# A pooled attention and a gated convolutional FFN on one core: the whole written-out order of operations is replaced

## The chip, the core and the metric

The kernel runs on one core of one Trainium2 chip. The metric is the device time of one execution in microseconds. The engines are TensorE (PE; its weight loads are listed as PEld), VectorE (DVE), ScalarE (ACT), GpSimd (POOL) and SyncE (SP). Each runs its own instructions strictly in the order in which the program issued them, and waits on semaphores for the others.

## The reference

There are 8 batches of 576 rows, 8 heads of 64. Keys and values are averaged over groups of 8 rows, so that 576 queries meet 72 pooled keys. The attention's output (576 x 512 a batch) goes through a feed-forward layer whose hidden activation (1024 wide) is multiplied by a sigmoid gate, which is a three-tap convolution along the sequence.

```python
k_p = k.reshape(B, H, Sp, pool, D).mean(axis=3)
v_p = v.reshape(B, H, Sp, pool, D).mean(axis=3)
scores = scale * np.matmul(q, k_p.transpose(0, 1, 3, 2))
attn = softmax(scores)                       # over 72 keys
x = np.matmul(attn, v_p)                     # heads side by side: 576 x 512
h = np.maximum(x @ w_in, 0.0)                # 576 x 1024
conv_out = sum(conv_w[k] * hp[:, k:k + S, :] for k in range(3))
out = (h * sigmoid(conv_out)) @ w_out        # 576 x 512
```

## The kernel before, in words

Batches go in pairs, the groups g = 0 to 3 (batches 2g and 2g + 1), and a group's 1152 rows are cut into tiles t of 128 rows (tile 4 holds the seam of both batches; group 0 has two halves of it, tiles 4 and 9). POOL issues all loads of inputs and weights: `load_q` and `load_k` (L272), `load_v` (L290 and a rest at L293), `load_pair` for the keys of a whole group (L279), `load_w_in` in two halves (L300) and `load_w_out` (L308). SP and ACT issue the stores, and SP the transposing DMAs.

One attention tile is a chain over the engines: scores on PE (`att_scores`, L567 in a form of 64 x 64 tiles, or L580), the negative maximum on DVE (L593), the shift by it (DVE L605, or for group 0 PE L613), exp on ACT (L631), the turning of e (on PE, L642, with a copy, L656; from group 2 on by a transposing DMA that SP issues, L651), the values on PE (`att_values`, L667), the division on DVE (L680, L682), and the turning into xT (PE L699 and a copy, L707, or a DMA, L691).

One batch's FFN has, for each of eight blocks of 128 hidden columns, the first product on PE (`ffn_in`, L712), relu on ACT (L721), the convolution (either on PE by diagonal matrices, L874, or as three taps, ACT L847 and DVE L849), tanh on ACT (L854, L899), the gate and its product with h on DVE (L860, L861, L910, L912, L920), then the second product (`ffn_out`, L928), a copy out of PSUM (L939, DVE or ACT) and the store (L951).

Before the first tile, PE averages and turns batch 0's keys with a pool matrix (L391; the matrix is made by DVE memsets at L327 to L329, two POOL selects at L316 and a DVE copy at L332) and turns its queries (L501). For later groups DVE sums the key pair in three halving steps (`pool_pair`, L424) and the values in three steps and a masked product (L471, L475).

The function builds a list of 1013 operations with their dependences, but decides nothing about their order. That is written out in three tables in the class `Graph`. `ORDER` holds one number for each operation in the order of issue: the half of it is the operation's index, the lowest bit chooses the first or the second engine that it may use, and -1 is a filler, a matmul of 448 columns on a blank tile whose result nobody reads (L384). `FORMS` chooses between two tilings of some score and turning operations on PE. `PLACES` gives each use of a ring of buffers (PSUM banks, e, eT, v, qp and others) its slot. The operations are emitted in that order, and so every engine's queue is a subsequence of it:

```python
for n in self.ORDER:
    o = spares.pop(0) if n < 0 else self.ops[n // 2]
    o.engine = list(o.engines)[0 if n < 0 else n % 2]
```

Of the kernel before, what the change touches and what calls it, by code (L numbers as in the profile page):

```python
# [33 lines left out]
class Graph:  # L34
# [88 lines left out]
    )  # L123
    FORMS = (
        1, 1, 0, 0, 0, 1, 1, 0, 0, 0, 0, 0, 1, 1, 1, 0, 0, 0, 0, 0, 0, 1, 1, 0, 0, 0, 0, 0, 0, 0, 0, 1, 1, 1, 0, 1, 1, 1, 1, 1,
    )
    PLACES = (
# [1265 lines left out]
```

## Time and profile before

| what | value |
|---|---|
| median of 3 runs | 222.53 us (221.14 to 223.88) |
| the profiled execution | span 224.8 us; no time beside the span is shown |
| PE busy | 205.1 us, 91% |
| DVE busy | 195.4 us, 87% |
| ACT busy | 160.9 us, 72% |
| POOL busy | 45.1 us, 20% |
| mean granted TensorE clock | 0.979 |

A busy time is the union of an engine's instructions. Matmuls are pipelined and their ends are modelled, so a busy PE need not be at its peak. "Idle before" in a group's row is the time for which its engine stood ahead of it, with what ended that; "issue" is a wait for nothing that the profile shows. The granted clock is that of TensorE, where 1 is full speed.

### The profile page before, as it was taken

The numbers are of one execution on the slowest core, as the hardware profiler recorded it, in microseconds if no ns is written. First come the engines' busy times: TensorE is split into PE (matmuls) and PEld (weight loads), VectorE is DVE, ScalarE is ACT, GpSimd is POOL, SyncE is SP. The second block draws the span as 40 slices with busy tenths as digits, with TensorE's granted clock in tenths as the row PEclk, the third lists the DMA queues.
The fourth block names the chain that finished last, engine by engine and source line by source line (L and its number), as shares of the span: only waits on it lengthen the run. The fifth ranks groups of instructions, "written<-read, shape, count | busy, mean of one in ns | idle before, by whom it ended". The sixth has DMA issues, their size and how long they took to land.

```text
span 224.8 us, 6558 instructions
## 1 busy us (share of the span) xinstructions
PE 205.1 (91%) x2722; PEld 137.9 (61%) x2722; DVE 195.4 (87%) x337; ACT 160.9 (72%) x271; POOL 45.1 (20%) x81
## 2 busy tenths in 40 slices
PE   5897999979999999959999949989999999999991
PEld 1465778755788877636677735656656665654450
DVE  7889876999999999957999948999999999999641
ACT  2155768898999958844697935688889999997210
POOL 7943321131230120000000121001031230540000
PEclk9999999999999999988999988999999999999997
DMA  5999999999999999947664553168566617423495
GB/s 81 137 191 207 207 206 208 207 207 206 207 208 206 155 187 172 207 39 163 121 106 92 119 118 76 32 92 165 117 145 140 137 23 166 95 48 71 96 247 194
DMA packets 48833, 32.61 MB, mean 145 GB/s; under 512 B 28300, under 2 KB 44324, under 8 KB 48804
## 3 DMA queue, kind: packets, MB, share of 16 engines
q0 software_dynamic: 16288, 16.26, 44.8%
q1 hardware_dynamic: 31796, 14.96, 33.3%
q10 hardware_dynamic: 720, 0.98, 1.5%
q8 instruction: 21, 0.34, 0.6%
q14 instruction: 8, 0.07, 0.1%
HBM read 32.52 MB, written 9.44 MB: 187 GB/s over the span
## 4 chain that ended last, share of the span: by engine, by line
PE 44%; DVE 30%; DMA 8%; issue 7%; ACT 6%; POOL 3%; DVEq 0%; POOLq 0%
PE psum L928 21%; PE psum L712 14%; DVE negm L593 6%; DMA qp<-in_q_dram 6%; DVE x L682 5%; DVE sd L605 5%; PE psum L874 4%; DVE tg L849 2%; DVE gT L912 2%; PE psum L667 2%; DMA eT<-e 2%; DVE v L471 2%; DVE r L680 2%; DVE gT L920 2%; ACT e L631 1%
## 5 line engine op out<-in xcount | busy, mean ns | idle before, releaser
L712 PE MATMUL psum<-xT,w_in_sb 128*128 128x288 bf16 x512 | 74.4, 289 | 0.8 <-ACT tg L899 0.5
L928 PE MATMUL psum<-w_out_sb,gT 128*128 128x512 bf16 (+1 forms) x296 | 70.3, 378 | 0.5 <-DVE gT L920 0.5
L712 PEld LDWEIGHTS <-w_in_sb 128*128 128x128 bf16 x512 | 48.4, 99 | 17.6 <-issue 1.6
L721 ACT ACTIVATE hT<-psum 128x576 bf16<-128x576 f32 x64 | 40.1, 652 | 14.9 <-PE psum L712 14.3
L928 PEld LDWEIGHTS <-gT 128*128 128x128 bf16 x296 | 27.7, 98 | 27.0 <-issue 1.2
L849 DVE SCALAR_TENSOR_TENSOR tg<-hT,convw,tg 128x576 f32<-128x576 bf16 x48 | 37.3, 818 | 0.4
L593 DVE TENSOR_REDUCE negm<-psum 128x8 f32<-128x576 f32 (+2 forms) x37 | 27.4, 750 | 4.4 <-PE psum L567 3.9
L796 POOL COPY hT<-hT 128x126 bf16<-128x126 bf16 x16 | 9.1, 567 | 101.4 <-ACT hT L721 90.9
L682 DVE TENSOR_TENSOR x<-psum,r 128x512 bf16<-128x512 f32 (+1 forms) x37 | 25.6, 691 | 1.3
L667 PE MATMUL psum<-vm,eT 128*128 128x130 bf16 (+5 forms) x240 | 20.0, 227 | 4.1 <-DMA eT<-e 2.9
L874 PE MATMUL psum<-hT,dw 64*64 64x288 bf16 (+2 forms) x608 | 19.2, 261 | 2.6 <-issue 2.3
L667 PEld LDWEIGHTS <-eT 128*128 128x128 bf16 (+1 forms) x240 | 16.0, 103 | 9.1 <-DMA eT<-e 3.8
L605 DVE TENSOR_TENSOR sd<-psum,negm 128x576 f32<-128x576 f32 x27 | 20.1, 752 | 1.0 <-ACT e L631 0.5
L631 ACT ACTIVATE e<-sd 128x576 bf16<-128x576 f32 x27 | 18.6, 689 | 1.8 <-DVE sd L605 1.6
L874 PEld LDWEIGHTS <-dw 64*64 64x64 bf16 x608 | 14.8, 107 | 7.6 <-issue 6.7
L847 ACT ACTIVATE tg<-hT,convw 128x576 f32<-128x576 bf16 x24 | 18.0, 773 | 1.0 <-DVE gT L912 0.9
L899 ACT ACTIVATE tg<-psum 128x576 bf16<-128x576 f32 x20 | 13.0, 653 | 7.2 <-PE psum L874 7.2
L939 ACT COPY osb<-psum 128x512 f32<-128x512 f32 x25 | 14.5, 586 | 4.0 <-PE psum L928 3.9
L854 ACT ACTIVATE gT<-tg 128x576 bf16<-128x576 f32 x24 | 16.2, 685 | 0.8 <-DVE tg L849 0.3
L471 DVE TENSOR_TENSOR v<-v 128x1280 bf16<-128x1280 bf16 (+2 forms) x24 | 13.0, 540 | 2.1 <-DMA v<-in_v_dram 1.9
L899 ACT ACTIVATE gT<-psum 128x576 bf16<-128x576 f32 x20 | 12.9, 649 | 2.0 <-PE psum L874 2.0
L920 DVE TENSOR_TENSOR gT<-gT,hT 128x2304 bf16<-128x2304 bf16 x10 | 13.5, 1349 | 0.0
(82 smaller groups left out, 236.2 us busy)
## 6 DMA issues: line engine op xcount, KB each, us to landing
out_dram<-osb SPq DMA_DIRECT2D x54, 128.0 KB, 2.4
v<-in_v_dram POOLq DMA_DIRECT2D x8, 512.0 KB, 15.2
qp<-in_q_dram POOLq DMA_DIRECT2D x7, 576.0 KB, 16.9
kk<-in_k_dram POOLq DMA_DIRECT2D x3, 1152.0 KB, 17.6
out_dram<-qp SPq DMA_DIRECT2D x10, 128.0 KB, 2.9
w_in_sb<-in_moe_w_in_dram POOLq DMA_DIRECT2D x2, 512.0 KB, 17.3
w_out_sb<-in_moe_w_out_dram POOLq DMA_DIRECT2D x1, 1024.0 KB, 24.3
out_dram<-qp ACTq DMA_DIRECT2D x6, 128.0 KB, 2.7
```

Of the source, the lines that this page charges most:

```text
L593: nc.vector.tensor_reduce(out=a["m"][0:rows], in_=a["s"][0:rows, :, 0:2 * KW].rearrange("p a (h s) -> p a h s", s=Sp), axis=AX.X, op=OP.ma ...
L605: nc.vector.tensor_tensor(out=a["d"][0:rows], in0=a["s"][0:rows, :, 0:2 * KW].rearrange("p a (h s) -> p a h s", s=Sp), in1=a["m"][0:rows]. ...
L631: nc.scalar.activation(out=dst, in_=src, func=ACT.Exp, scale=1.0 / (POOL * 8.0),)
L667: nc.tensor.matmul(out=a["o"][lo:hi, h // 4, (h % 4) * (D + 1):(h % 4 + x1 - x0) * (D + 1)], lhsT=a["eT"][:, j, lo:hi], rhs=buf("vm", b)[: ...
L682: nc.vector.tensor_tensor(out=a["x"][0:rows].rearrange("p (a h d) -> p a h d", a=2, d=D), in0=ov[:, :, :, 0:D], in1=r[0:rows].unsqueeze(3) ...
L712: nc.tensor.matmul(out=banks(ps)[:, j, 0:SC], lhsT=w_in_block(dc, fb), rhs=buf("xT", g)[:, dc, i * S + j * SC:i * S + (j + 1) * SC], start ...
L721: nc.scalar.activation(out=h_of(b)[:, fb].rearrange("p (a s) -> p a s", a=2), in_=banks(ps)[:, :, 0:SC], func=ACT.Relu, scale=0.5,)
L847: nc.scalar.activation(out=acc, in_=h, func=ACT.Identity, scale=w)
L849: nc.vector.scalar_tensor_tensor(out=acc, in0=h, scalar=w, in1=acc, op0=OP.mult, op1=OP.add)
L874: nc.tensor.matmul(out=banks(pss[r ^ c])[c * D:(c + 1) * D, j, lo:hi], lhsT=dw[r * D:(r + 1) * D, tap * n_fb + fb, :], rhs=hT[r * D:(r + 1 ...
L899: nc.scalar.activation(out=t.rearrange("p (a s) -> p a s", a=2), in_=banks(ps)[:, :, 0:SC], func=ACT.Tanh, scale=0.5,)
L928: nc.tensor.matmul(out=bank(ps)[0:rows, columns], lhsT=buf("gT", g)[:, fb, t * P:t * P + rows], rhs=w_out_sb[:, fb, columns], start=(fb == 0),
```

## The change

Only the three tables are replaced. The same 1013 operations are issued in another order; 15 stand at the place in the list that they had (fillers not counted), and the mean shift is 21 places, the largest 167. 28 copies change between DVE and ACT (17 from DVE to ACT, 11 back), and 7 stores between SP and ACT. 22 fillers become 2. In `FORMS`, one more turning of queries and one more score operation use the small tiling. All line numbers move up by 18, since the tables are shorter: L712 is now L694, and so on. The first rows of `ORDER` and the whole of `FORMS`:

```diff
     ORDER = (
-        18, 24, 2, 6, 4, 8, 10, -1, 16, -1, 14, -1, 20, 22, 12, -1, 42, -1, 44, -1,
-        -1, 34, 28, -1, 36, -1, -1, 30, 32, -1, 92, 0, 96, 98, 38, 95, -1, 56, 26, 104,
+        6, 10, 2, 4, 28, 16, 14, 20, 24, 22, 34, 8, 26, 42, 36, 44, 12, 32, 30, 40, 92, 56, 18, 98, 38, 95, 58, 101, 104, 64,
+        97, 108, 103, 106, 50, -1, 110, 54, 48, 302, 282, 60, 116, 304, 112, 119, 284, 306, 114, 286, 308, -1, 288, 322, 342, 324, 310, 66, 344, 326,
...
     FORMS = (
-        1, 1, 0, 0, 0, 1, 1, 0, 0, 0, 0, 0, 1, 1, 1, 0, 0, 0, 0, 0, 0, 1, 1, 0, 0, 0, 0, 0, 0, 0, 0, 1, 1, 1, 0, 1, 1, 1, 1, 1,
+        1, 1, 0, 0, 0, 1, 1, 1, 0, 1, 0, 1, 0, 1, 1, 0, 0, 0, 0, 0, 1, 1, 0, 0, 0, 0, 1, 1, 1, 1, 0, 0, 1, 0, 1, 0, 1, 0, 1, 0,
...
```

What this moves is seen in the queues of the engines. First POOL's loads after those of batch 0, before. The names are buffers: qp holds a batch's queries (qp1 to qp3 here batches 1 to 3, the qp0 below them batch 4), kk keys, v values of one batch, w_in_sb0 and 1 the halves of w_in.

```order
L272 DMA qp1_73<-in_q_dram 128x4x576
L272 DMA qp2_74<-in_q_dram 128x4x576
L300 DMA w_in_sb0_66<-in_moe_w_in_dram 128x4x512
L300 DMA w_in_sb1_67<-in_moe_w_in_dram 128x4x512
L290 DMA v1_86<-in_v_dram 128x4x512
L293 DMA v1_86<-in_v_dram 64x512
L279 DMA kk0_76<-in_k_dram 128x9x512
L272 DMA qp3_75<-in_q_dram 128x4x576
L272 DMA qp0_72<-in_q_dram 128x4x576
L308 DMA w_out_sb_68<-in_moe_w_out_dram 128x8x512
L290 DMA v2_87<-in_v_dram 128x4x512
L293 DMA v2_87<-in_v_dram 64x512
```

And now:

```order
L254 DMA qp1_73<-in_q_dram 128x4x576
L254 DMA qp2_74<-in_q_dram 128x4x576
L282 DMA w_in_sb1_67<-in_moe_w_in_dram 128x4x512
L282 DMA w_in_sb0_66<-in_moe_w_in_dram 128x4x512
L272 DMA v1_86<-in_v_dram 128x4x512
L275 DMA v1_86<-in_v_dram 64x512
L272 DMA v2_87<-in_v_dram 128x4x512
L275 DMA v2_87<-in_v_dram 64x512
L261 DMA kk0_76<-in_k_dram 128x9x512
L254 DMA qp0_72<-in_q_dram 128x4x576
L254 DMA qp1_73<-in_q_dram 128x4x576
L290 DMA w_out_sb_68<-in_moe_w_out_dram 128x8x512
```

Batch 2's values have moved ahead of the key pair of group 1 (kk0), of the queries of batches 4 (qp0) and 3 (now in qp1, and behind batch 4's) and of w_out; the halves of w_in have changed places.

Next PE's queue ahead of the values of tile (2, 5), group 2's tile 5. Of runs of equal rows the first is shown. xT0 is group 2's input to the FFN, eT its turned exponentials. Before, after the values of tile (2, 6), which read eT1; those of tile (2, 5) read eT0:

```order
L667 MATMUL psum_61<-vm0_88,eT1_103 128x65
L712 MATMUL psum_61<-xT0_112,w_in_sb1_67 128x288
L712 MATMUL psum_61<-xT0_112,w_in_sb0_66 128x288
L667 MATMUL psum_61<-vm0_88,eT2_104 128x130
L667 MATMUL psum_61<-vm0_88,eT0_102 128x130
```

And now, after the values of tile (2, 7); those of tile (2, 5) read eT2:

```order
L694 MATMUL psum_61<-xT1_113,w_in_sb1_67 128x288
L694 MATMUL psum_61<-xT0_112,w_in_sb1_67 128x288
L856 MATMUL psum_61<-hT0_114,dw_71 64x288
L549 MATMUL psum_61<-kT2_82,qT2_79 64x72
L910 MATMUL psum_61<-w_out_sb_68,gT0_119 128x512
L649 MATMUL psum_61<-vm0_88,eT0_102 128x130
L649 MATMUL psum_61<-vm1_89,eT2_104 128x130
```

Where two tiles' values stood next to each other behind some products of one batch, the values of tile (2, 5) now come behind products of two batches, a convolution, scores of group 3, output products and the values of a tile of group 3. Counted from the tile's own scores to its values, PE had 36 L712 matmuls and two tiles' values to do; now it has 72 of them (L694), 16 of L928 (L910), four convolution groups (128 matmuls of L874, now L856), 48 matmuls of scores and four tiles' values. The shortest such stretch of a tile of groups 2 and 3 is now that of tile (3, 1): 20 of L712, 16 of L928, one convolution group of 24 and 32 score matmuls.

Last, PE's start, before:

```order
L384 LDWEIGHTS gT1_120
L384 MATMUL psum_61<-gT1_120 128x448
L365 MATMUL psum_61<-gT1_120 128x24
L391 LDWEIGHTS kk0_76
L391 MATMUL psum_61<-gT1_120,kk0_76 64x144
```

And now:

```order
L347 MATMUL psum_61<-gT1_120 128x24
L373 LDWEIGHTS kk0_76
L373 MATMUL psum_61<-gT1_120,kk0_76 64x144
L483 LDWEIGHTS qp0_72
L483 MATMUL psum_61<-ident_62,qp0_72 64x128
```

Eleven fillers (L384) stood ahead of the first key matmul (L391) and eleven more came later; now none stands ahead of it, and the two that are left come after the first turnings of queries (L483) and among the first tiles' shifts.

116 rows, old and new, of tables (ORDER, PLACES) are left out of this document.

## The prediction

> **What bounds the kernel now.** I read the page first: busy shares and the chain that ended last.
>
> ```profile
> span 224.8 us, 6558 instructions
> PE 205.1 (91%) x2722; PEld 137.9 (61%) x2722; DVE 195.4 (87%) x337; ACT 160.9 (72%) x271; POOL 45.1 (20%) x81
> PE 44%; DVE 30%; DMA 8%; issue 7%; ACT 6%; POOL 3%; DVEq 0%; POOLq 0%
> ```
>
> TensorE (PE) is busy for 91% and VectorE (DVE) for 87%, and both carry the chain. The order of the work can only win what these two lose by waiting for each other or for transfers. Where that is, the busy time of each engine in seven stretches tells. After the stretch and its length come the busy times, the granted TensorE clock, the DMA share and GB/s.
>
> ```profile
> core 0: us, PE busy (x) PEld busy (x) DVE busy (x) ACT busy (x) POOL busy (x), PEclk, DMA share, GB/s
> 0.00:28.00 28.00, 22.05 (x387) 14.46 (x390) 23.63 (x59) 12.89 (x21) 16.18 (x33) 1.00 1.06 165
> 28.00:95.30 67.30, 64.83 (x1119) 49.37 (x1106) 62.77 (x113) 57.48 (x100) 11.84 (x17) 1.00 1.21 198
> 95.30:104.40 9.10, 6.81 (x97) 3.96 (x100) 5.13 (x9) 3.59 (x8) 0.00 (x0) 0.81 0.52 74
> 104.40:125.20 20.80, 20.63 (x400) 15.28 (x388) 20.26 (x38) 15.87 (x28) 0.00 (x0) 1.00 0.60 115
> 125.20:145.10 19.90, 17.02 (x187) 11.40 (x176) 15.62 (x26) 12.50 (x21) 3.32 (x8) 0.91 0.45 94
> 145.10:216.10 71.00, 70.09 (x574) 41.21 (x563) 65.68 (x93) 57.98 (x98) 13.77 (x24) 1.00 0.52 113
> ```
>
> In three of them both engines are nearly full (PE 64.83 of 67.30, 20.63 of 20.80 and 70.09 of 71.00): no order wins much there. The loss sits in the start, and in two short stretches where PE stands and the granted clock is below 1. The waits of PE between 90 and 140 us name two gaps, with the total, the times and the longest:
>
> ```profile
> PE psum L667 <- DMA eT<-e: 2.9, 1, 2.9
> PE psum L874 <- issue: 2.3, 1, 2.3
> ```
>
> The same table, cut finely around them, shows that a gap costs more than its length:
>
> ```profile
> 92.59:96.01 3.42, 3.42 (x80) 2.17 (x78) 3.29 (x5) 2.62 (x6) 0.00 (x0) 1.00 1.06 181
> 96.01:99.42 3.41, 1.12 (x35) 0.83 (x34) 0.65 (x2) 1.00 (x2) 0.00 (x0) 1.00 0.63 35
> 99.42:102.84 3.42, 3.42 (x16) 1.74 (x15) 2.70 (x5) 1.28 (x4) 0.00 (x0) 0.50 0.17 34
> 130.14:133.55 3.41, 0.54 (x8) 0.34 (x5) 1.11 (x2) 0.98 (x2) 1.26 (x2) 1.00 0.60 131
> 133.55:136.97 3.42, 3.41 (x18) 2.42 (x19) 2.47 (x5) 0.00 (x0) 0.00 (x0) 0.50 0.30 60
> 48.22:51.63 3.41, 2.50 (x62) 1.56 (x64) 3.38 (x5) 3.37 (x7) 0.77 (x1) 1.00 1.23 206
> ```
>
> PE was busy for 1.12 of 3.41 us, and then for 0.54 of 3.41 us, and each time the next 3.41 us ran at a clock of 0.50. Such a half-speed stretch does 1.7 us less work. So the first gap costs 2.3 + 1.7 = 4.0 us and the second 2.9 + 1.7 = 4.6 us. A stretch with 2.50 of 3.41 us busy (48.22) was followed by no loss of clock.
>
> By the Trainium skill, "TensorE: Matmul & The Clock Gate", Part 1, the clock halves after an idle window of about 3.4 us, and the windows run freely. The trace agrees, with 3413 ns to the window.
>
> **The change, part by part.** All 1013 planned operations stay; their order, their buffers, 35 choices of engine and some tiling forms change. Of 22 filler matmuls on PE 2 stay. The sum is made against the profiled execution's 224.8 us. Its row shows nothing around the span, and it is 1.0% above the median of the timed runs (222.53), so I scale the result by 0.990.
>
> *(a) The start without fillers.* The fillers take 7.8 us of PE, beside DVE's start and the first loads.
>
> ```profile
> L384 PE MATMUL psum<-gT 128*128 128x448 bf16 x22 | 7.8, 463 | 2.8 <-DVE gT L1027 2.5 <-ACT eT L656 0.2
> 4.08 3.17 PE L384 MATMUL psum<-gT 128*128 128x448 bf16 x8
> 8.32 1.32 PE L391 MATMUL psum<-gT,kk 128*64 128x144 bf16 x36 [1.07 <-DVE gT L332]
> 9.86 0.64 PE L501 MATMUL psum<-ident,qp 128*64 128x128 bf16 x16
> 10.43 0.55 PE L384 MATMUL psum<-gT 128*128 128x448 bf16 x2
> ```
>
> Eight early ones took 3.17 us (0.40 each), two later ones 0.55 (0.28 each): the early ones ran slowly and the key and query work after them did not. Without them L391 (1.32 us) and L501 (0.64) are the first long work and may take twice that, +2.0 us. Against it, DVE clears the pool matrix first and four other buffers earlier, so that L332 may come sooner; PE waited 1.1 us for it, and no more can be won. I take +0.8, between -1.1 and +2.0.
>
> The same page puts the warm-up at about 3.4 us at half speed, whatever is issued. By that alone this term would be +1.7 and the result 0.9 us later.
>
> *(b) The load queue.* Batch 2's values now go ahead of the key pair of batches 2 and 3.
>
> ```profile
> 28.00:40.00 12.00, 11.94 (x207) 9.60 (x197) 8.71 (x20) 8.72 (x16) 3.03 (x5) 1.00 1.24 207
> 20.64 1.03 POOL L279 DMA_DIRECT2D kk<-in_k_dram  x1 [4.75 <-PE psum L401]
> kk<-in_k_dram POOLq DMA_DIRECT2D x1, 1152.0 KB, 17.8
> 39.46 1.35 DVE L424 TENSOR_TENSOR kk<-kk 128x2304 bf16<-128x2304 bf16 x1
> ```
>
> The pair lands at 20.64 + 17.8 = 38.4 us, and DVE sums it at 39.46. Batch 2's 576 KB take 2.8 us at 207 GB/s, so it lands at 41.2 now: DVE waits up to 1.8 us at the head of its queue, with the scores' maxima behind it. But v2's own four operations now stand ahead of that sum and fill part of the wait. I take the middle, +0.9, between 0 and +1.8.
>
> *(c) The transposing DMA of tile (2, 5).* This is the second gap; the two rows of x4 are from the chain's listing, the others from the timeline.
>
> ```profile
> 124.95 0.32 PE L567 MATMUL psum<-kT,qT 64*64 64x72 bf16 x16
> 129.13 1.22 SPq L651 DMA_TRANSPOSE eT<-e  x1
> 133.56 0.84 PE L667 MATMUL psum<-vm,eT 128*128 128x130 bf16 x6 [2.88 <-DMA eT<-e]
> 34.12 0.49 PE psum L712 x4
> 82.21 0.86 PE psum L928 x4
> 124.14 0.94 PE L874 MATMUL psum<-hT,dw 64*64 64x288 bf16 x32
> 127.35 0.52 PE L667 MATMUL psum<-vm,eT 128*128 128x130 bf16 x6
> ```
>
> From the end of its scores (125.3) to its values (133.6) lie 8.3 us: maximum, shift, exp, sending, landing. PE had 36 L712 matmuls (9 x 0.49) and two other tiles' values (2 x 0.52) to do between, 5.4 us; so it stood 2.9. The new order puts 72 L712, 16 L928, four conv groups and four tiles' values there, beside 48 score matmuls: 8.8 + 3.4 + 3.8 + 2.1 = 18 us without the scores. That covers 8.3, and 4.6 us go. The shortest such cover is now that of tile (3, 1): 20 L712 (2.5), 16 L928 (3.4), one conv group (0.9) and two groups of scores (0.6), 7.4 us. Where its chain also takes 8.3, PE stands 0.9, too short for the clock to fall; I take +0.4, and the term is -4.2, between -4.6 and 0 (if another tile comes late).
>
> *(d) Engines.* 17 copies go from DVE to ACT and 11 come back.
>
> ```profile
> L519 DVE COPY qT<-psum 128x1152 bf16<-128x1152 bf16 (+2 forms) x6 | 3.9, 648 | 0.7 <-PE psum L501 0.7
> L939 DVE COPY qp<-psum 128x512 f32<-128x512 f32 (+1 forms) x6 | 3.6, 601 | 5.6 <-PE psum L928 5.3 <-DMA out_dram<-qp 0.2
> L416 DVE CAST kT<-psum 64x144 bf16<-64x144 f32 (+1 forms) x5 | 1.8, 366 | 0.9 <-PE psum L391 0.8
> ```
>
> Net, five key casts (0.37), one query copy (0.65) and two output copies (0.60) leave DVE, and one or two short copies of 0.4 come: some 3 us less. ACT at 72% takes it. After 145 us PE is full, so most of it is hidden; I take -0.6, between -3 and 0.
>
> *(e) The first gap.* In the middle of a conv group PE waited for nothing that the profile shows. I cannot say what the order has to do with it, and leave it in: 0, between -4.0 and 0.
>
> Sum: 224.8 + 0.8 + 0.9 - 4.2 - 0.6 = 221.7 us, times 0.990 = **219.5 us**, 1.4% under the median. All low ends together give 224.8 - 1.1 - 4.6 - 3 - 4.0 = 212.1, or 210.0; all high ends 224.8 + 2.0 + 1.8 = 228.6, or 226.3.
>
> **The rivals.** *Both gaps close.* For it: the first comes where conv groups stand densely among scores, and in the new order that region is thinner. Against: nothing shows its cause. 221.7 - 4.0 = 217.7, or 215.5 us.
>
> *A new gap opens.* Two in 190 us came in an order as full as this. Any wait of some 2.3 us in one window would do, as for the loads of (b) or for batch 3's queries, now two loads later. For it: slack is short everywhere. Against: the shortest cover of a tile grew from 5.4 to 7.4 us. 221.7 + 4.6 = 226.3, or 224.0 us.
>
> *The start falls back to half speed* (the slower side). What the fillers did from 10.68 to 14.09 us, theirs alone and then all:
>
> ```profile
> 10.68:14.09 3.41, 1.39 (x7) 0.48 (x5) 1.00 1.13 164
> 10.68:14.09 3.41, 3.03 (x65) 1.90 (x64) 2.97 (x6) 1.50 (x3) 2.54 (x4) 1.00 1.13 164
> ```
>
> Without them 1.64 of 3.41 us stay busy, 48%. That lies between the 33% that halved the clock and the 73% that did not. If it decides against the kernel, PE's 22.05 us up to 28 us less 7.5 for the 21 fillers there, 14.6 us of real work, take 14.6 more; DVE is busy for 23.63 of the 28, so 4.4 are hidden and 10.2 pass on: 221.7 - 0.8 + 10.2 = 231.1, or 228.8 us. Against: at half speed the same work fills the window, and the clock would come back after one of them. By the page's table only an idle window sends it back, and then this case would not occur; no row here shows 48%.
>
> *The order makes no difference*: gaps come and go with the chip's state, and 222.5 stays.
>
> **How the numbers follow.** The forecast has a chance of 0.32, both gaps closed 0.25, a new gap 0.20, the slow start 0.14, no difference 0.09. A measurement of this kernel tells about 2% from no change; that is 218.1 and 227.0 us. The forecast lies near the lower of these and gives a third of its chance to faster (0.11). With both gaps closed (0.25) that makes 0.36. Slower comes from the slow start (0.13) and from more than one new gap (0.07): 0.20. The rest is 0.44. The range runs from 214.0, below the case of both gaps closed, to 227.5, above that of a new gap; the forecast's own is 217 to 222.
>
> **What would show it.** In the profile of the changed kernel: no wait of L667 for eT above 1 us (c); the first key matmuls about twice 1.32 us long, and the first L712 matmul near 29 us, as now at 29.3 (a); DVE waiting for kk at 40 us (b); DVE busy some 3 us less (d). Stretches with a clock of 0.50 tell the cases apart: none after the start means both gaps closed, one the forecast, two or more a new gap, several before 28 us the slow start. The prediction is wrong in its core if a wait above 2.3 us stands on PE before the values of some other tile.

## The result, and the profile after

The changed kernel takes 218.34 us (median of 6, 218.08 to 218.71), the kernel before in the same comparison 222.11 us (median of 6). The ratio is 0.9876, with an interval of 0.9834 to 0.9918: 1.2% faster, and less than the 2% that the prediction named as the bound. 219.5 us was predicted, with a range of 214.0 to 227.5. The profiled execution of the new order took 218.51 us for a span of 216.8, so 1.7 us lie outside the span. The ratios here and below leave out executions that lie more than 1.5% above the fastest of their kernel; the medians hold all.

The head of its page, and the two stretches that had a clock under 1 (PE, PEld, DVE, ACT and POOL busy, then the clock):

```profile
span 216.8 us, 6589 instructions
PE 196.2 (91%) x2718; PEld 136.2 (63%) x2736; DVE 191.3 (88%) x331; ACT 164.3 (76%) x277; POOL 46.8 (22%) x81
PE 75%; DVE 9%; ACT 5%; issue 3%; POOL 3%; DMA 2%; DVEq 0%; POOLq 0%; ACTq 0%
```

```profile
95.30:104.40 9.10, 7.95 (x119) 5.22 (x122) 8.16 (x16) 6.89 (x13) 0.00 (x0) 1.00 0.71 153
125.20:145.10 19.90, 19.80 (x291) 13.62 (x282) 19.33 (x32) 16.12 (x28) 4.68 (x10) 1.00 0.61 107
```

The clock is whole in both (0.81 and 0.91 before), and between 125 and 145 us PE now works 19.80 of 19.90 us. The chain lies on PE for 75% of the span, where it was 44%. (18 matmul records are missing here, 2718 against 2736 weight loads; the second profile of this order, below, has all.) Three of the waits of PE, with total, times and longest, and three rows of its timeline:

```profile
PE psum L373 <- DVE gT L314: 4.3, 1, 4.3
PE psum L562 <- ACT kT L425: 0.6, 1, 0.6
PE psum L412 <- DVE kk L406: 0.4, 1, 0.4
8.48 2.37 PE L373 MATMUL psum<-gT,kk 128*64 128x144 bf16 x36 [4.34 <-DVE gT L314]
28.59 0.65 PE L694 MATMUL psum<-xT,w_in_sb 128*128 128x288 bf16 x4
96.33 0.53 PE L649 MATMUL psum<-vm,eT 128*128 128x130 bf16 x6 [0.99 <-DMA eT<-e]
```

The only wait for a transposing DMA left stands at 96 us. After 97 us PE waits nowhere for more than 0.2 us. This looks like the rival with both gaps closed, which asked for a span of 217.7; and yet the time fell by 3.8 us, not by the 8 us that lie between the two spans. So the first thing to settle is what the first profile of the kernel before had shown.

### The profile page after: what moved, and what is told of

Same layout as the page of the kernel before. It is cut to its first block, busy times and chain, and to the rows that moved or that the text cites. A ratio compares the mean times of both kernels' runs of the same rounds, so it can differ in the third digit from the quotient of the medians.

```text
span 216.8 us, 6589 instructions
## 1 busy us (share of the span) xinstructions
PE 196.2 (91%) x2718; PEld 136.2 (63%) x2736; DVE 191.3 (88%) x331; ACT 164.3 (76%) x277; POOL 46.8 (22%) x81
## 3 DMA queue, kind: packets, MB, share of 16 engines
q10 hardware_dynamic: 880, 1.25, 2.1%
## 4 chain that ended last, share of the span: by engine, by line
PE 75%; DVE 9%; ACT 5%; issue 3%; POOL 3%; DMA 2%; DVEq 0%; POOLq 0%; ACTq 0%
PE psum L910 28%; PE psum L694 26%; PE psum L649 6%; PE psum L856 5%; DVE negm L575 3%; DMA eT<-e 2%; PE psum L624 2%; PE psum L549 2%; ACT qT L501 1%; DVE sd L587 1%; PE psum L681 1%; PE psum L562 1%; ACT eT L638 1%; PE psum L373 1%; PE psum L595 1%
## 5 line engine op out<-in xcount | busy, mean ns | idle before, releaser
L694 PE MATMUL psum<-xT,w_in_sb 128*128 128x288 bf16 x512 | 72.4, 286 | 0.1
L910 PE MATMUL psum<-w_out_sb,gT 128*128 128x512 bf16 (+1 forms) x278 | 66.2, 373 | 0.9 <-issue 0.2
L694 PEld LDWEIGHTS <-w_in_sb 128*128 128x128 bf16 x512 | 47.8, 98 | 15.6 <-issue 0.2
L910 PEld LDWEIGHTS <-gT 128*128 128x128 bf16 x296 | 27.5, 98 | 26.1 <-issue 0.5
L649 PE MATMUL psum<-vm,eT 128*128 128x65 bf16 (+5 forms) x240 | 19.3, 222 | 1.4 <-DMA eT<-e 1.0
L856 PE MATMUL psum<-hT,dw 64*64 64x288 bf16 (+2 forms) x608 | 19.4, 261 | 0.5 <-DVE sd L587 0.3
L856 PEld LDWEIGHTS <-dw 64*64 64x64 bf16 x608 | 15.4, 107 | 5.2 <-issue 4.3
L649 PEld LDWEIGHTS <-eT 128*128 128x128 bf16 (+1 forms) x240 | 15.1, 100 | 5.3 <-DMA eT<-e 1.2
L453 DVE TENSOR_TENSOR v<-v 128x1280 bf16<-128x1280 bf16 (+2 forms) x24 | 13.0, 541 | 0.3
```

The source lines that it names most:

```text
L649: nc.tensor.matmul(out=a["o"][lo:hi, h // 4, (h % 4) * (D + 1):(h % 4 + x1 - x0) * (D + 1)], lhsT=a["eT"][:, j, lo:hi], rhs=buf("vm", b)[: ...
L694: nc.tensor.matmul(out=banks(ps)[:, j, 0:SC], lhsT=w_in_block(dc, fb), rhs=buf("xT", g)[:, dc, i * S + j * SC:i * S + (j + 1) * SC], start ...
L856: nc.tensor.matmul(out=banks(pss[r ^ c])[c * D:(c + 1) * D, j, lo:hi], lhsT=dw[r * D:(r + 1) * D, tap * n_fb + fb, :], rhs=hT[r * D:(r + 1 ...
L910: nc.tensor.matmul(out=bank(ps)[0:rows, columns], lhsT=buf("gT", g)[:, fb, t * P:t * P + rows], rhs=w_out_sb[:, fb, columns], start=(fb == 0),
```

## The experiments

In the rewritten tables line numbers move: in e1, e2 and e4 they stand ten lower than in the kernel before (L702 is L712), in e3 twelve lower; e5 to e7 have those of the kernel before, and e8 to e12 those of the new order. "Before" in a ratio is always the kernel before on the same chip.

**e1: the kernel before once more.** No edit.

> The kernel before, unchanged, to see what its executions have in common. Theory (gaps come and go): the two gaps of the first profile are not in every execution. Each half-speed stretch of 3.41 us lowers the mean clock by about 0.5 x 3.41 / 224 = 0.008, so executions near 219.5 us should show a mean clock of 0.99 or more and those near 224 about 0.98; a new profile should lack at least one of the two gaps if its span is under 221 us. Rival (both gaps are a property of the order): the mean clock stays within 0.003 of the 0.979 of the first profile in every execution, both waits (2.3 us in the convolution, 2.9 us for eT) stand in the new profile, and what spreads the times from 219.5 to 223.9 lies elsewhere.

Measured: 223.0 us (median of 12, 220.0 to 226.24). The profiled execution took 221.78 us for a span of 220.0:

```profile
span 220.0 us, 6558 instructions
PE 201.9 (92%) x2722; PEld 136.5 (62%) x2722; DVE 195.1 (89%) x337; ACT 161.1 (73%) x271; POOL 45.2 (21%) x81
PE psum L864 <- issue: 1.2, 1, 1.2
PE psum L657 <- DMA eT<-e: 0.8, 2, 0.5
```

Both gaps are there, but 1.2 us in place of 2.3 and 0.5 in place of 2.9, and no half-speed stretch follows either. The transfer of tile (2, 5)'s exponentials took 2.59 us from issue to landing here and 4.38 us in the first profile, which is most of the difference of the second gap; what made it slow there stays open. With the kernel before of all comparisons in which clocks are listed there are 113 executions of it, sorted here by their mean granted clock:

| mean clock | executions | median us |
|---|---|---|
| 0.9935 and above | 72 | 220.84 |
| 0.9905 to 0.9935 | 11 | 221.11 |
| 0.9815 to 0.9905 | 25 | 223.41 |
| under 0.9815 | 5 | 226.17 |

One half-speed stretch lowers the mean clock by 0.5 x 3.41 / 222 = 0.008, so by this reckoning the third row holds executions with one, the fourth with two. (In e1's profile, with its 0.995, the only half speed stands behind PE's last matmul.) The profile that the prediction worked from, with its clock of 0.979 and two such stretches, is of the kind that 5 of 113 executions are. The theory that gaps come and go holds in part: it expected one of the two to be missing, and both are there; what comes and goes is their length and the half-speed stretch behind them.

**e9: the new order once more.** No edit.

> The new order once more, unchanged, for its spread and a second profile. The kernel before spread over 219.5 to 226.2 us, with mean clocks from 0.978 to 0.998. Theory (the new order leaves PE no gap long enough to halve the clock): all executions lie within 1 us of 218.3 and no mean clock is under 0.99. Rival (six executions were too few to see it): some executions lie above 220 us, with a clock under 0.99.

Measured: 218.8 us (median of 12, 217.84 to 221.86), ratio 0.9909 [0.9878, 0.9939]; the first ratio is confirmed. Eleven executions lie within 217.8 to 219.5, one at 221.86 with a clock of 0.987, so the rival has a point: a half-speed stretch still comes at times, perhaps behind the gap at 96 us, of which no profile was taken. Over both sets that is 1 of 18 executions, where it is 30 of 113 for the kernel before. The means are 218.7 and 221.8 us; without a half-speed stretch they are 218.5 (17 executions) and 221.0 (the first row's 72). So of 3.1 us the rarer half-speed stretches are some 0.6, and 2.5 are in every execution.

Where that rest lies, the two ordinary executions tell, first e1, then e9:

```profile
core 0: us, PE busy (x) PEld busy (x) DVE busy (x) ACT busy (x) POOL busy (x), PEclk, DMA share, GB/s
28.00:95.30 67.30, 64.11 (x1117) 49.43 (x1117) 62.23 (x112) 57.13 (x98) 11.71 (x17) 1.00 1.20 198
95.30:120.00 24.70, 23.23 (x388) 16.15 (x390) 22.49 (x41) 17.26 (x31) 0.00 (x0) 1.00 0.64 110
120.00:150.00 30.00, 28.58 (x403) 19.15 (x396) 28.55 (x48) 23.79 (x40) 5.07 (x12) 1.00 0.63 114
204.62 10.18 PE L918 MATMUL psum<-w_out_sb,gT 128*128 128x512 bf16 x54
```

```profile
span 217.1 us, 6607 instructions
28.00:95.30 67.30, 64.19 (x1164) 50.04 (x1152) 63.20 (x109) 58.98 (x99) 12.02 (x20) 1.00 1.18 194
95.30:120.00 24.70, 23.45 (x344) 15.94 (x342) 23.13 (x41) 17.53 (x31) 0.00 (x0) 1.00 0.63 122
120.00:150.00 30.00, 30.00 (x412) 21.04 (x411) 29.18 (x52) 24.07 (x41) 5.21 (x12) 1.00 0.57 109
204.78 7.52 PE L910 MATMUL psum<-w_out_sb,gT 128*128 128x512 bf16 x42
```

PE idles the same 3.1 to 3.2 us in the long second stretch. It wins 0.2 us up to 120 us and 1.4 us from there to 150, where it never stands now. Behind 150 us e9's PE does not stand either, up to its end; e1's stands for 0.4 us. PE ends at 214.8 us in e1 and 212.3 in e9, and what follows its end is 5.2 and 4.8 us.

**e2: the second gap alone.** SP sends tile (2, 5) ahead of tile (2, 7)'s x, and its values come four groups of L712 later. In words of the operations:

```diff
 SP:  send eT (2, 8)
+SP:  send eT (2, 5)
 SP:  send x (2, 7)
-SP:  send eT (2, 5)
 PE:  values (2, 8)
-PE:  values (2, 5)
 PE:  4 groups of L712
+PE:  values (2, 5)
```

> The kernel before with the second gap alone repaired: the values of tile (2, 5) and its division come four groups of four L712 matmuls later (2.0 us), and SP issues the transposing DMA of its exponentials ahead of that of tile (2, 7)'s x (up to 1.2 us earlier). Theory (step c, the gap is on the path in every execution): PE's wait for eT shrinks from 2.9 us to under 1 us, the half-speed stretch behind it goes, and the time falls by 4.6 us, to about 217.5 from a median of 222.1. Theory (gaps come and go): the fall is the gap's share in the executions only, 1 to 3 us. Rival (DVE, busy for 87%, carries the end anyway): less than 1 us.

Measured: 221.41 us, ratio 0.9986 [0.9949, 1.0024], that is -0.3 us (-1.1 to +0.5). The rival stands: the wait for eT went, and another came behind it, of an output product for tile (2, 5)'s division on DVE.

```profile
PE psum L918 <- DVE x L672: 1.0, 1, 1.0
```

**e5: four tiles.** As e2 with two groups of L712 for (2, 5), one group for (3, 2), and the sends of (3, 3) and (3, 6) one place earlier on SP.

```diff
+SP:  send eT (3, 3)
 SP:  send x (3, 2)
-SP:  send eT (3, 3)
+SP:  send eT (3, 6)
 SP:  store
-SP:  send eT (3, 6)
```

> The kernel before with more time for four transposing DMAs of exponentials. In its second profile the values of tiles (2, 5), (3, 2), (3, 3) and (3, 6) start 2.6 to 2.7 us after SP starts to issue their DMA, so PE stands each time by what the DMA is late (0.5, 0.6 and 0.3 us there, 2.9 us at (2, 5) in the first profile). Here SP issues three of these DMAs one place earlier in its queue, and the values of (2, 5) and (3, 2) come two and one groups of L712 later. Theory (tight transfers make the kernel slow and unsteady): PE's gaps after 120 us fall from 1.4 us to under 0.4, the median falls by 1.2 to 2 us, and executions with a mean clock under 0.99 become fewer. Rival (what PE wins there is lost to DVE or at the next tile): the median moves by less than 0.6 us.

Measured: 221.78 us, ratio 1.0071 [1.0034, 1.0108], 1.6 us slower. No wait for eT of 0.2 us or more is left, and PE waits for DVE's shifts in its place:

```profile
PE psum L712 <- DVE sd L605: 0.8, 1, 0.8
PE psum L874 <- DVE sd L605: 0.7, 1, 0.7
```

So the time that these transfers were given here won nothing. DVE is nearly full there (28.55 of 30.00 us in e1), and values that come later on PE hold up the divisions in its queue, as in e2. That this is the whole of the 1.6 us was not shown; faster transfers with PE's order left alone were not tried.

**e3: no fillers at the start.**

```diff
-        18, 24, 2, 6, 4, 8, 10, -1, 16, -1, 14, -1, 20, 22, 12, -1, 42, -1, 44, -1,
+        18, 24, 2, 6, 4, 8, 10, 16, 14, 20, 22, 12, 42, 44,
...
```

> The kernel before without its first 20 filler matmuls; the last two stay. Step a of the prediction: +0.8 us (-1.1 to +2.0), key matmuls L391 near 2.4 us long in place of 1.32. Rival (the start falls back to half speed): +10 us. A third theory, on the first gap: PE's instructions are fetched in blocks while it runs, and the gap in the convolution at 96 us is a block that came late; 40 fewer instructions on PE then move the block's border by some 40 instructions, and the 2.3 us wait leaves its place in L874. If the gap has to do with the order of work around it, it stays where it was, 2.3 us long.

Measured: 221.2 us, ratio 0.9992 [0.9955, 1.0029], that is -0.2 us (-1.0 to +0.6). The key matmuls took 2.37 us, as expected, and the start did not fall back for good: the clock halved for one stretch from 16.23 us (rows in the last section). The third theory's test is in PE's timeline around 96 us, first e1, then e3:

```profile
96.01 0.68 PE L864 MATMUL psum<-hT,dw 64*64 64x288 bf16 x17
97.88 0.53 PE L864 MATMUL psum<-hT,dw 64*64 64x288 bf16 x13 [1.19 <-issue]
```

```profile
95.68 0.94 PE L862 MATMUL psum<-hT,dw 64*64 64x288 bf16 x32
96.45 0.22 PE L555 MATMUL psum<-kT,qT 64*64 64x72 bf16 x5
97.86 0.29 PE L555 MATMUL psum<-kT,qT 64*64 64x72 bf16 x11 [1.19 <-issue]
```

In the first profile, in e1, e2 and e5 PE stopped after the 17th matmul of that convolution group. With 20 matmuls fewer ahead it stopped exactly 20 matmuls later, in other work: the 15 that the group had left and 5 of the scores. So this gap belongs to a place in PE's instruction stream, not to an operation or a buffer. It does not come each time: e4 has the same matmuls in the same order, and there PE passed the place at 98.6 us, some 2 us later than in the others, without a stop.

**e6: fewer instructions there.** The larger tiling for the two turnings of batch 5's queries and the scores of tiles (1, 1) and (2, 7), four entries of `FORMS`:

```diff
-form 1 (64 x 64): turning (5, half 0), turning (5, half 1), scores (1, 1), scores (2, 7)
+form 0 (128 rows): the same four
```

> The kernel before with four PE operations between 78 and 98 us in their larger tiling (both turnings of batch 5's queries and the scores of tiles (1, 1) and (2, 7)): 60 matmuls and 60 weight loads fewer of some 390 rows there, PE busy some 0.4 us more. The first gap stood at matmul 1501 of the trace in the kernel before and, with 20 matmuls fewer ahead, again at 1501, 20 operations later in the program. Theory (a block of instructions comes late because PE eats small instructions faster than they are brought): with fewer instructions to eat the gap shrinks below 0.5 us wherever the border now lies, and the time falls by 0.5 to 1.5 us. Rival (the border costs 1.2 to 2.3 us whatever stands ahead of it): the gap stands again at matmul 1501, now 60 matmuls later in the program, as long as before, and the time is 0.4 us more.

Measured: no wait for "issue" of 0.2 us or more is left in the profile; the first gap is gone. One profile cannot tell that the edit did it, since e4's shows no gap there either; the last section has more on this. The profiled execution was this kernel's fastest, 218.87 us, but the median is 221.13 and the ratio 1.0024 [0.9993, 1.0056]. 2 of 12 executions have a mean clock under 0.9905, and 4 of 20 of the kernel before on that chip, so it is not clearly steadier either. The expected 0.5 to 1.5 us did not come.

**e7: e5 and e6 together.** No further edit.

> Both edits together in the old order: time for four transposing DMAs, and the four larger tilings. If these two mechanisms are what the new order does better, the median comes to within 0.7 us of the new order's 218.3, from some 221.5. If the new order wins elsewhere (the start, DVE's work, the end), it stays above 220.

Measured: 222.02 us, ratio 1.0060 [1.0030, 1.0090]. Both gaps are closed in its profile and the kernel is slower. PE waits for DVE's shift (L605) for 0.9, 0.8, 0.7 and 0.6 us, where e5 had 0.8, 0.7, 0.6 and 0.2. Closing the two gaps on which the prediction turned, in this way, does not give the new order's gain.

**e4: the 28 choices of engine in the old order.** Of `ORDER`'s numbers the lowest bits alone change, for the keys of batch 0 for instance (numbers that stand between them left out):

```diff
-        100, 96, 102   (key copies of batch 0: DVE)
+        101, 97, 103   (ACT)
...
```

> The kernel before, in its own order, with only the 28 changed choices between DVE and ACT of the new tables (17 copies from DVE to ACT, 11 back). Step d: DVE busy some 3 us less (195.4 to about 192.4), ACT some 3 us more, the time 0.6 us less (0 to 3). Rival (the choices belong to the new order, and in the old one the copies now wait in ACT's queue): 1 to 3 us more, with PE waiting for ACT's copies.

Measured: 223.35 us, ratio 1.0057 [1.0016, 1.0098], 1.3 us slower (0.4 to 2.2), though DVE's busy time fell as expected, from 195.1 to 192.5 us. The rival's time came, but PE's longest new wait is for a key copy that DVE took over, not for one of ACT's:

```profile
PE psum L570 <- DVE kT L433: 1.0, 1, 1.0
```

**e8: the old 28 choices in the new order.** The edit of e4 turned round.

```diff
-        101, 97, 103
+        100, 96, 102
...
```

> The new order with the 28 choices between DVE and ACT of the kernel before. Those choices of the new tables cost 1.3 us (0.4 to 2.2) in the old order. Theory (step d, less DVE work helps): DVE busy 3 us more and 0.6 us more time, 0 to 3. Rival 1 (choices are good or bad only with their order): 1 us more or above. Rival 2 (the new choices are bad in themselves): about 1 us less than the new order's 218.3.

Measured: 222.89 us, ratio to before 1.0121 [1.0090, 1.0151], 4.1 us above the 218.8 of e9, which ran on another chip; by the two ratios it is 4.7. The whole gain of the new order is gone, and more. Rival 1 holds: the choices are good in one order and bad in the other. "Order" here is all the rest of the new tables: the seven stores that change their engine and the other tilings were not tried alone.

**e10: the first 20 of them alone.** As e8, but the eight copies of the last outputs keep the new engine.

> The new order with the choices between DVE and ACT of the kernel before for the 20 copies that stand in the first half of the list (keys, queries, turned exponentials, up to 100 us); the eight of the last output copies keep the new choices. All 28 together cost 4.5 us. Theory (the start and the middle are paced by DVE, and the first copies stand in its way there): 3 to 4.5 us more than 218.3, with PE's progress behind by 1.5 us at the first L694. Rival (the output copies at the end make it): under 1.5 us more.

Measured beside e9: 222.05 us against 218.8, ratio to before 1.0045 [1.0009, 1.0080] against 0.9909. So 3.2 us, most of the whole, come from the first half. DVE's timeline at the start, first e9, then e10:

```profile
12.52 1.42 DVE L575 TENSOR_REDUCE negm<-psum 128x8 bf16<-128x576 f32 x2
14.93 1.42 DVE L575 TENSOR_REDUCE negm<-psum 128x8 bf16<-128x576 f32 x2 [0.59 <-PE psum L562]
24.97 1.42 DVE L575 TENSOR_REDUCE negm<-psum 128x8 bf16<-128x576 f32 x2 [0.21 <-PE psum L549]
```

```profile
10.90 0.85 DVE L398 CAST kT<-psum 64x144 bf16<-64x144 f32 x3 [0.62 <-PE psum L373]
15.75 1.42 DVE L575 TENSOR_REDUCE negm<-psum 128x8 bf16<-128x576 f32 x2 [1.05 <-PE psum L562]
21.80 0.93 DVE L398 CAST kT<-psum 64x288 bf16<-64x288 f32 x2
26.20 1.42 DVE L575 TENSOR_REDUCE negm<-psum 128x8 bf16<-128x576 f32 x2
```

Three key casts stand ahead of the first maxima, and the third and fourth maximum come 0.82 us later (15.75 against 14.93). Two more stand between the divisions, and the maxima of tiles 7 and 8 come 1.23 us later (26.20 against 24.97). PE follows, first e9, then e10:

```profile
28.60 0.65 PE L694 MATMUL psum<-xT,w_in_sb 128*128 128x288 bf16 x4
48.05 0.41 PE L562 MATMUL psum<-kT,qT 128*128 128x144 bf16 x4 [0.55 <-ACT kT L425]
96.61 0.53 PE L649 MATMUL psum<-vm,eT 128*128 128x130 bf16 x6 [1.25 <-DMA eT<-e]
```

```profile
30.33 0.65 PE L694 MATMUL psum<-xT,w_in_sb 128*128 128x288 bf16 x4
49.94 0.41 PE L562 MATMUL psum<-kT,qT 128*128 128x144 bf16 x4 [1.03 <-ACT kT L425]
99.65 0.53 PE L649 MATMUL psum<-vm,eT 128*128 128x130 bf16 x6 [0.69 <-DMA eT<-e]
```

The first product of the FFN comes 1.7 us later, where 1.5 was expected, and the next two groups 1.9 and then 3.0 us. In both kernels PE is busy for all 30.00 us from 120 to 150 and waits nowhere after its last wait near 100 us, so the 3.0 us are handed on to the end (span 220.4 against 217.1).

**e11: the keys ahead of the values again, in the new order.**

```diff
 POOL: load v1
+POOL: load kk0 (group 1)
 POOL: load v2
-POOL: load kk0 (group 1)
 DVE:  division (0, 6)
+DVE:  pair sum step 0, division (0, 7), steps 1 and 2
 DVE:  divisions (0, 9), (0, 5)
+DVE:  values of batch 2, four operations
```

> The new order with the key pair of group 1 loaded ahead of batch 2's values again, and with DVE's three sums of that pair 2 to 3 us earlier in its queue, ahead of the four operations on batch 2's values. Step b of the prediction (the load order costs 0.9 us, 0 to 1.8): 0.9 us less than 218.3, and PE's waits of 0.4 us for L406 and 0.6 us for the key copies at 45 to 48 us go. Rival (DVE is full there, and what one sum wins another operation loses): within 0.5 us of 218.3. Rival (batch 2's values now come late): more, with a wait of DVE at L453.

Measured: 221.33 us against e9's 218.8, ratio to before 1.0049 [1.0006, 1.0092]; 2.5 us slower. The wait for L406 went, but a copy of xT on DVE came late, and the clock fell in the window behind it:

```profile
PE psum L681 <- DVE xT L689: 1.3, 1, 1.3
46.33:49.74 3.41, 1.35 (x36) 1.17 (x36) 3.28 (x8) 2.90 (x7) 2.29 (x3) 1.00 1.24 207
49.74:53.16 3.42, 3.29 (x58) 3.06 (x57) 3.38 (x6) 2.15 (x3) 0.75 (x1) 0.50 1.24 206
```

DVE is busy for 3.28 of 3.41 us there: what its sum wins, its other operations lose, which is the first rival's reason, but the time is the second's, without the wait at L453 that it named. The four operations on batch 2's values now stand at 45.28 to 47.6 us, ahead of that copy at 49.39. All executions but one have a mean clock under 0.99; that one, at 1.0, took 221.05 us, so the half-speed stretch is not what makes this kernel slow. The wait of 0.6 us for the key copies stayed.

**e12: fillers in the new order.** Ten ahead of the first key matmul.

```diff
-PE:  L347, L373 (first keys)
+PE:  L347, ten of L366, L373 (first keys)
```

> The new order with ten filler matmuls ahead of the first key matmul, where PE waits 4.3 us for the pool matrix; DVE clears the tile they read one place earlier. In both profiles of the new order the first key matmuls take 2.37 us at half speed, against 1.32 behind the fillers of the old order. Theory (the full clock at the start is worth what the first keys gain): L373 1.32 us, the first maximum on DVE 1 us sooner, the time 0.7 to 1.2 us less, about 217.5. Rival (DVE and the loads pace the first 28 us): L373 1.32 us, and within 0.5 us of 218.5.

Measured: 219.15 us, ratio 0.9927 [0.9894, 0.9961], against 0.9909 without. The rival's time is near: 0.35 us above e9's median, and no gain. The keys took 1.64 us in place of 2.37, the first maxima came 0.94 us sooner, and the end did not. At 25.65 us PE stood for 1.0 us in its own instruction stream (first row), as in neither profile without the fillers; whether the fillers cause this stop, one profile does not tell:

```profile
PE psum L562 <- issue: 1.0, 1, 1.0
8.48 1.64 PE L373 MATMUL psum<-gT,kk 128*64 128x144 bf16 x36 [0.49 <-DVE gT L314]
```

No version of these beat the new order.

## Why the number was right and most of its steps were not

**The base.** The step that failed first is the scaling by 0.990. It treats the profiled execution as an ordinary one that is 1% long in all its parts. The 224.8 us are also a span, to which some 1.7 us come outside it (e1, e9 and the first result agree on that), so that its time was nearer 226.5 us, 1.8% above the median. The execution was a rare one, long in two places: two gaps that with their half-speed stretches cost 8.6 us there and 1.7 us (1.2 and 0.5) in e1. The sum then took one of these gaps off a base from which the scaling had already taken part of it.

**(c) -4.2 us: wrong.** The gap of tile (2, 5) did go, and tile (3, 1) with the shortest cover does not appear among PE's waits. But the gap is 0.5 us in e1, and its repair alone gave -0.3 us (e2). The price of one execution was taken for that of all. The cover on PE was not the measure either: the wait that is left in the new order, 0.99 and 1.25 us at 96 us, is that of tile (2, 3), which has 72 L694 matmuls and five convolution groups between scores and values; its transfer took 4.26 us from issue to landing in e9, against 2.6 for most. (The cover of tile (3, 1) was summed a little long: a convolution group of 24 takes 0.7 us by the row of 32.)

**(e) 0 us, the first gap left in.** It closed in the new order too. Its place in the instruction stream is shown (e3), and that it does not come in every execution of the same stream (e4). That e6's edit closed it is likely, not shown. A block of instructions that arrives late fits the stops in the traces (last section). Without the gap the old order won nothing in the median (e6).

**(a) +0.8 us: size wrong, details right.** The keys took 2.37 us as said, and the first L694 came at 28.59 us, 0.7 earlier than before. The fillers are worth -0.2 us (-1.0 to +0.6) in the old order, and nothing that can be measured in the new one. The slow start came in neither profile of the new order; in e3's, one window with PE busy for 2.05 of 3.41 us (60%) was followed by one half-speed stretch, which ended by itself, as the prediction's "against" had it.

**(b) +0.9 us: the wait did not come.** The keys landed at 40.7 us, 2.2 us later than before, where 2.8 was reckoned. DVE reached their sum at 41.42 us with nothing idle ahead of it:

```profile
41.42 1.35 DVE L406 TENSOR_TENSOR kk<-kk 128x2304 bf16<-128x2304 bf16 x1
```

What the later sum costs shows on PE, as the 0.4 us for L406 and 0.6 us for the key copies. e11 undid the load order together with DVE's order, so the price of the loads alone stays open.

**(d) -0.6 us: the term that was mis-sized.** DVE's busy time fell by 4.1 us, some 3 were expected. The step reasoned that PE is full after 145 us and hides most of it. That may hold for the eight output copies: e8 less e10 is 0.8 us by the medians and 1.7 by the ratios, of two comparisons. But 20 of the 28 copies stand ahead of 100 us, where DVE paces the tiles, and those are worth 3.2 us in the new order (e10) while all 28 cost 1.3 us in the old one (e4). So the sum of parts that the prediction formed does not exist: the choices and the rest of the tables pay only together.

By the signs that the prediction named (no clock of 0.50 after the start, no long wait for eT) the case that came was its rival with both gaps closed, priced at 215.5 us. That the forecast of 219.5 us came near 218.3 is luck, since two errors offset each other: a gap priced at 4.6 us that ordinarily costs little, and a gain of some 3 us through DVE that was priced at 0.6. Which rows of the new order give the 1.4 us between 120 and 150 us was not isolated; the runs show that PE does not wait there, and that the same holds with the old choices of engine (e10), so this part is the order's own.

## What to carry to other kernels

Before a gap in a profile is priced, look at whether the profiled execution is an ordinary one: its mean clock beside that of the other executions, and its time beside their median, tell it at once. Here, where two engines are nearly full, closing the first one's waits (for a DMA, for instructions) won nothing (e2, e5 to e7). Choices of engine have to be judged with the order in which they will run: the same 28 cost 1.3 us in one and were worth about 4 in the other. What a copy moved ahead of DVE's chain at the start saved was kept to the end, since PE hardly waits from 100 us on in that order (e10).

## What the runs showed of the hardware

PE's stops for "issue" of 0.2 us and more stand on a grid of its instruction stream. Counted in matmuls from the kernel's start they come after 350 (e12), 478 (all profiles of the new order itself, e11 and e12), 1373 (e1, e2) and 1501 (the first profile, e1, e2, e3, e5), in programs and operations that differ. The first two and the last two places lie 128 matmuls apart, and 895 lie between, one short of 7 x 128. 128 matmuls with their 128 weight loads are 256 instructions. The page counts the instruction transfers:

```profile
q8 instruction: 21, 0.34, 0.6%
```

These are 21 packets of 16 KB, so one would hold 256 instructions of 64 bytes (an estimate). Their times in the traces fit as well. In all twelve stops counted here PE went on 1.29 to 1.64 us after the end of such a packet. Where it passed one of these four places without standing, it came there 1.51 us or more after such an end: in e4, with the first profile's stream, 1.68 us, where in e1 it came after 0.1 us and stood until 1.29; and in e6 3.5 us. So a stop looks like the rest of the time that a block of instructions needs, where small matmuls use up the block before it too fast. That is a match of times; no row names what PE waited for.

The clock can halve without an idle window. A window with PE busy for 1.35 of 3.41 us was followed by 0.50 (e11), and so was one with 2.05 (e3, first row below), while one with 1.86 (e9, third row) was not, nor was one with 1.66 (e7, 5.71 to 9.13 us):

```profile
12.82:16.23 3.41, 2.05 (x30) 1.20 (x27) 3.23 (x5) 1.62 (x3) 0.45 (x2) 1.00 1.20 200
16.23:19.65 3.42, 3.42 (x27) 2.85 (x26) 3.17 (x6) 2.42 (x5) 0.46 (x1) 0.50 1.20 204
```

```profile
93.25:96.66 3.41, 1.86 (x57) 1.43 (x55) 3.36 (x4) 3.35 (x7) 0.00 (x0) 1.00 1.10 105
96.66:100.07 3.41, 3.41 (x52) 2.14 (x53) 2.58 (x6) 1.16 (x3) 0.00 (x0) 1.00 0.98 215
```

The Trainium skill, "TensorE: Matmul & The Clock Gate", Part 1, has the clock fall after at least one idle window of about 3.4 us. The length of the window agrees (3.41 us in these rows); but ahead of these falls no window was idle, and the busy share alone does not decide either.
